# Attention normalised as it leaves PSUM, own banks for the last output parts, and scores ahead of the last image sums

## The chip, the cores and the metric

The kernel runs on one core of a Trainium2 chip. The metric is the device time of one execution in microseconds (us), as a median of several. Beside it stands the span of one profiled execution, which is some 2 us shorter than the time of the same execution.

## The reference

Spatial-reduction attention is followed by a gated feed-forward layer. The image `kv` (4 x 384 x 32 pixels of 128 channels) is averaged over 4 x 4 pixels and projected to 768 keys per batch, which are the values too. The feed-forward layer has two products of width 1536.

```python
k = v = kv_pool.reshape(B, -1, C) @ w_sr
a = softmax(q @ k.transpose(0, 2, 1) / sqrt(C))      # B=4, N=12288, C=128
x = (a @ v).reshape(B * N, C)
out = (maximum(x @ w_gate, 0) * (x @ w_val)) @ w_out  # 128 -> 1536 -> 128
```

If x is scaled by s per row, both factors of the last line are, and the output by s squared. Both kernels use that.

## The kernel before

The 49152 rows are worked in 96 tiles of 512. In a tile there are six score products and exponentials, 24 small products for the attention's output (with a column of ones beside the values, which gives the sums), 12 value products, 12 gate products, and 12 sets of 4 output products. Attention runs ahead of the feed-forward part by three tiles, and the work of both is interleaved in 12 steps per tile. Every PSUM tile is one of eight banks; what TensorE writes goes to PSUM, the other tiles lie in SBUF. In the names of tiles below, `aT` are the exponentials, `x` the attention output, `val` and `hT` the value factor and the gated product, `o_sb` the output, `rinv` the reciprocal sums. The attention output stays unnormalised, and the output is scaled by the square of the reciprocal sums:

```python
def keep_values(k, half, copy=nc.vector.tensor_copy, now=True):
    own = slice(2 * half, 2 * half + 2)
    x_ps = x_banks.pop((k, half))
    copy(x16s[k][:, own, :], x_ps[:, :, 0:C])            # L205
    sums[k, half] = x_ps[:, :, C]
    if now:
        keep_sums(k, half)

def keep_sums(k, half):
    nc.vector.reciprocal(rinvs[k][:, 2 * half : 2 * half + 2], sums.pop((k, half)))   # L211
    if half == 0:
        return
    ...
    nc.vector.tensor_tensor(inv2s[k][:, :, 0], rinv, rinv, op=ALU.mult)               # L216

# out_scale: ScalarE with inv2 as pointer, 4 of 128x128, or VectorE:
    nc.vector.tensor_tensor(o_sbs[k][:, own, :], o_banks[k][:, own, :],
        inv2s[k][:, own].to_broadcast([128, own.stop - own.start, 128]), op=ALU.mult)  # L274

# out_last: one bank for the four parts of the last tile
    o_banks[k] = bank([128, NS, 128])
    ...   # parts 0 and 1, scaled and stored together; then parts 2 and 3, one by one

# first full tile (k == LAG): ScalarE copies four half tiles out
    values(kV, jc, half)
    if jc == NJC - 1:
        keep_values(kV, half, nc.scalar.copy)
```

At the start, the last third of the image is summed and transposed (L153) before the scores of the second third:

```python
project(0, 1)
turn_open(0, 2)
turn_add(0, 2, s2, first=True)       # transposes of the first two rows' sums
for k in range(GRP):
    for jc in range(2, 4):
        scores(k, jc)
    ...
    if k == 1:                       # sums of the last two rows, and their transposes
        for h in range(2):
            s2 = add_lines(2, 2, nc.vector, slice(h, h + 1))
            turn_add(0, 2, s2, final=True, chunks=[h])
```

The softmax here doesn't subtract the row's maximum and nothing guards it: scores larger than these inputs give would overflow.

Of the kernel before, what the change touches and what calls it, by code (L numbers as in the profile page):

```python
# [9 lines left out]
FP32 = mybir.dt.float32  # L10
FP16 = mybir.dt.float16
AF = mybir.ActivationFunctionType
ALU = mybir.AluOpType
# [3 lines left out]
def kernel(  # L17
# [22 lines left out]
    nc = tc.nc  # L40

    B, N, C = q.shape
# [6 lines left out]
    NFB = D_FF // 128  # L49
    T = 512  # L50
    NS = T // 128
# [2 lines left out]
    GRP = 4  # L54
    NG = NT // GRP
    LAG = GRP - 1
    qk_scale = 1.0 / math.sqrt(C)

    assert C == 128 and N % T == 0 and J == 128 * NJC and D_FF == 128 * NFB
# [3 lines left out]
    work = ctx.enter_context(tc.tile_pool(name="work", bufs=2))  # L63
    psum = ctx.enter_context(tc.tile_pool(name="psum", bufs=8, space=bass.MemoryType.PSUM))

    def bank(shape, dtype=FP32):
        return psum.tile(shape, dtype, tag="bank", name="bank_ps")
# [50 lines left out]
    kv16 = const.tile([128, B, NJC, 2 * C + 4], FP16)  # L118
# [26 lines left out]
    def turn_open(b, pair):  # L145
        kv_Ts[b, pair] = bank([128, 2, 128])
# [27 lines left out]
        nc.vector.tensor_copy(kv16[:, b, 2 * pair : 2 * pair + 2, C : 2 * C], vt)  # L174


    aTs, x_banks, x16s, xTs, rinvs, inv2s, sums = {}, {}, {}, {}, {}, {}, {}
    hTs, o_banks, o_sbs, vals = {}, {}, {}, {}

    def scores(k, jc):  # L180
# [6 lines left out]
    def values(k, jc, half):  # L187
        if jc == 0:
            x_banks[k, half] = bank([128, 2, C + 1])
            if half == 0:  # L190
                x16s[k] = work.tile([128, NS, C], FP16, tag="x16", bufs=3, name="x16")
                rinvs[k] = work.tile([128, NS], FP32, tag="rinv", bufs=3, name="rinv")
        x_ps = x_banks[k, half]
        for i in range(2):
            s = 2 * half + i
            nc.tensor.matmul(  # L196
                x_ps[:, i, :], aTs[k][:, jc, s * 128 : (s + 1) * 128],
                kv16[:, k // NST, jc, C : 2 * C + 1],
                start=(jc == 0 and i == 0), stop=(jc == NJC - 1), skip_group_check=True,
            )  # L200

    def keep_values(k, half, copy=nc.vector.tensor_copy, now=True):
        own = slice(2 * half, 2 * half + 2)
        x_ps = x_banks.pop((k, half))
        copy(x16s[k][:, own, :], x_ps[:, :, 0:C])  # L205
        sums[k, half] = x_ps[:, :, C]
        if now:
            keep_sums(k, half)

    def keep_sums(k, half):  # L210
        nc.vector.reciprocal(rinvs[k][:, 2 * half : 2 * half + 2], sums.pop((k, half)))  # L211
        if half == 0:
            return
        rinv = rinvs.pop(k)
        inv2s[k] = work.tile([128, NS, 1], FP32, tag="inv2", bufs=8, name="inv2")
        nc.vector.tensor_tensor(inv2s[k][:, :, 0], rinv, rinv, op=ALU.mult)  # L216

    def x_turn(k):
        x16 = x16s.pop(k)
# [32 lines left out]
        if fb == NFB - 1:  # L252
            xTs.pop(k)

    def out_add(k, fb, s, first):
        nc.tensor.matmul(  # L256
            o_banks[k][:, s, :], hTs[k][:, fb, s * 128 : (s + 1) * 128], wo16[:, fb, :],
            start=first, stop=(fb == NFB - 1), skip_group_check=True,
        )

    def out_proj(k, fb):
        if fb == 0:
            o_banks[k] = bank([128, NS, 128])
        for s in range(NS):
            out_add(k, fb, s, fb == 0 and s == 0)

    def out_scale(k, engine, own):
        if k not in o_sbs:
            o_sbs[k] = work.tile([128, NS, 128], FP32, tag="o_sb", bufs=3, name="o_sb")
        if engine is nc.scalar:  # L270
            for s in range(own.start, own.stop):
                nc.scalar.mul(o_sbs[k][:, s, :], o_banks[k][:, s, :], inv2s[k][:, s])
        else:
            nc.vector.tensor_tensor(  # L274
                o_sbs[k][:, own, :], o_banks[k][:, own, :],
                inv2s[k][:, own].to_broadcast([128, own.stop - own.start, 128]), op=ALU.mult,
            )

    def out_store(k, own):
        nc.sync.dma_start(  # L280
            out[k // GRP * GRP * T : (k // GRP + 1) * GRP * T, :].rearrange(
                "(p i s) c -> i p s c", p=128, i=GRP
            )[k % GRP][:, own], o_sbs[k][:, own],
        )
        if own.stop == NS:
            for tiles in (hTs, o_banks, inv2s, o_sbs):
                del tiles[k]

    def out_last(k):
        o_banks[k] = bank([128, NS, 128])  # L290
        for s in range(2):
            for fb in range(NFB - 1):
                out_add(k, fb, s, fb == 0 and s == 0)
        for s in range(2):
            out_add(k, NFB - 1, s, False)
        out_scale(k, nc.vector, slice(0, 2))
        out_store(k, slice(0, 2))
        for s in range(2, NS):
            for fb in range(NFB):
                out_add(k, fb, s, False)  # L300
            out_scale(k, (nc.scalar, nc.vector)[s % 2], slice(s, s + 1))
        out_store(k, slice(2, NS))

    ctx.enter_context(tc.manual_schedule())
# [6 lines left out]
    make_identity(nc, ident)  # L311
    ident16 = const.tile([128, 128], FP16)
    nc.gpsimd.tensor_copy(ident16, ident)
    nc.gpsimd.memset(kv16[:, :, :, 2 * C : 2 * C + 4], 1.0)

    w_sr_f32 = const.tile([128, C], FP32)
    nc.sync.dma_start(w_sr_f32, w_sr)
# [8 lines left out]
    wo16 = const.tile([128, NFB, 128], FP16)  # L326
# [46 lines left out]
    for h in range(2):  # L373
        s2 = add_lines(1, 2, nc.vector, slice(h, h + 1))
# [3 lines left out]
    s2 = add_lines(2, 0, nc.vector, slice(1, 2))  # L378
# [5 lines left out]
    nc.gpsimd.dma_start(wo16, moe_w_out.rearrange("(fb f) c -> f fb c", f=128))  # L384
    q_load(2)
    project(0, 1)
    turn_open(0, 2)
    turn_add(0, 2, s2, first=True)
    for k in range(GRP):
        for jc in range(2, 4):  # L390
            scores(k, jc)
        if k == 0:
            turn_values(0, 1)
        if k == 1:
            for h in range(2):
                s2 = add_lines(2, 2, nc.vector, slice(h, h + 1))
                turn_add(0, 2, s2, final=True, chunks=[h])
        if k == 2:
            project(0, 2)
# [6 lines left out]
        scores(1, jc)  # L406
    attend(0, 2)
    for half in range(2):
        keep_values(0, half, now=False)
    for jc in range(4, NJC):  # L410
        scores(2, jc)
    x_turn_pe(0)
    for half in range(2):
        keep_sums(0, half)
    for jc in range(4, NJC):
        scores(3, jc)
    attend(1, 2)
    for half in range(2):
        keep_values(1, half)
    for jc in range(NJC - 2):  # L420
        values(2, jc, 0)
# [3 lines left out]

    last = NT + LAG - 1
    for k in range(LAG, last + 1):
        g, ph = divmod(k, GRP)
        if ph == 1:
            q_turn(g + 1)  # L430
            q_load(g + 2)
        b = k // NST + 1
        at = k % NST - (NST - NJC - 6)
        for step in range(NFB):
            kO, kF = k - LAG - 1, k - LAG
            half, i = divmod(step // 2, NJC // 2)
            if 0 <= kO:
                out_proj(kO, step)
                if step == NFB - 1 and k < last:
                    out_scale(kO, nc.vector if kF < NT - 2 else nc.scalar, slice(0, NS))  # L440
                    out_store(kO, slice(0, NS))
            if kF < NT:
                value_proj(kF, step)
            if k == LAG:
                own, left = left[:2], left[2:]
                for kV, jc, half in own:
                    values(kV, jc, half)
                    if jc == NJC - 1:
                        keep_values(kV, half, nc.scalar.copy)
                        if half == 1:  # L450
                            x_turn(kV)
            elif step % 2 == 0:
                if k < NT:
                    scores(k, step // 2)
            elif k > GRP and k - 1 < NT:
                values(k - 1, 2 * i, half)
                values(k - 1, 2 * i + 1, half)
                if i == NJC // 2 - 1:
                    keep_values(k - 1, half)
                    if half == 1:  # L460
                        x_turn(k - 1)
            if kF < NT:
                gate_proj(kF, step)
            if k == LAG and step == 2:
                x_turn_pe(1)
            if b < B:
                if step == 1 and 0 <= at < NJC and at % 2 == 0:
                    kv_load(b, at // 2)
                if step == 3 and 0 <= at - 2 < NJC:
                    pool_pixels(nc.gpsimd, b, (at - 2) // 2, at % 2)  # L470
                pair = (at - 5) // 2
                if at % 2 == 1 and 0 <= pair < NJC // 2:
                    if step == 2:
                        turn_open(b, pair)
                        turn_add(b, pair, s3s.pop((b, pair))[:, :, None], True, True)
                    if step == 4:
                        project(b, pair)
                    if step == 8:
                        turn_values(b, pair)
    out_scale(last - LAG - 1, nc.scalar, slice(0, NS))  # L480
    out_store(last - LAG - 1, slice(0, NS))
# [31 lines left out]
```

## Time and profile before

The first three runs gave 1050.52 us as their median.

| engine | busy us | share of the span |
|---|---|---|
| TensorE | 1035.6 | 99% |
| VectorE | 920.5 | 88% |
| ScalarE | 909.5 | 87% |
| GpSimd | 107.8 | 10% |

TensorE bounds the kernel. So the useful way is to cut the span at three TensorE instructions that both kernels have: the first value product, the first score of the next stage, and the last value product. Lines of the timeline of before (start us, duration us, engine, line, operation, out<-in):

```profile
32.81 0.38 PE L235 MATMUL bank_ps<-xT,wv 128*128 128x512 f16 x1
...
40.91 0.38 PE L184 MATMUL bank_ps<-qT,kv 128*128 128x512 f16 x1
...
1040.22 0.38 PE L235 MATMUL bank_ps<-xT,wv 128*128 128x512 f16 x1
```

This makes four stretches: start (to 32.81), first full tile (40.91 - 32.81 = 8.10), steady stage (1040.22 - 40.91 = 999.31) and tail (1048.8 - 1040.22 = 8.58). The groups by line that the change replaces (busy us, mean ns, then idle time before them):

```profile
L205 DVE CAST x<-bank_ps 128x256 f16<-128x256 f32 x188 | 77.7, 414 | 0.9 <-PE bank_ps L196 0.8
L274 DVE TENSOR_TENSOR o_sb<-bank_ps,inv 128x512 f32<-128x512 f32 x93 | 63.2, 680 | 0.0
```

### The profile page before, as it was taken

The numbers are of one execution on the slowest core, as the hardware profiler recorded it, in microseconds if no ns is written. First come the engines' busy times: TensorE is split into PE (matmuls) and PEld (weight loads), VectorE is DVE, ScalarE is ACT, GpSimd is POOL, SyncE is SP. The second block draws the span as 40 slices with busy tenths as digits, with TensorE's granted clock in tenths as the row PEclk, the third lists the DMA queues.
The fourth block names the chain that finished last, engine by engine and source line by source line (L and its number), as shares of the span: only waits on it lengthen the run. The fifth ranks groups of instructions, "written<-read, shape, count | busy, mean of one in ns | idle before, by whom it ended". The sixth has DMA issues, their size and how long they took to land.

```text
span 1048.8 us, 26047 instructions
## 1 busy us (share of the span) xinstructions
PE 1035.6 (99%) x9980; PEld 688.8 (66%) x9980; DVE 920.5 (88%) x1776; ACT 909.5 (87%) x1743; POOL 107.8 (10%) x127
## 2 busy tenths in 40 slices
PE   7999999999999999999999999999999999999998
PEld 5666666666666666666666666666666666666665
DVE  3888889898989898988989898989888888989897
ACT  2988888888888888888888888888888888888886
POOL 2000045100000015400000003430000000000000
PEclk9999999999999999999999999999999999999999
DMA  8833356241322345523224144551331322212111
GB/s 298 132 71 83 81 176 157 51 87 32 87 56 62 71 129 143 152 52 71 67 51 87 32 86 132 151 147 47 72 78 41 77 60 56 62 34 64 32 46 47
DMA packets 125853, 90.75 MB, mean 87 GB/s; under 512 B 103328, under 2 KB 104224, under 8 KB 125728
## 3 DMA queue, kind: packets, MB, share of 16 engines
q1 hardware_dynamic: 120288, 75.85, 26.7%
q0 software_dynamic: 5440, 13.24, 7.8%
q8 instruction: 78, 1.28, 0.5%
q14 instruction: 47, 0.39, 0.1%
HBM read 52.76 MB, written 25.17 MB: 74 GB/s over the span
## 4 chain that ended last, share of the span: by engine, by line
PE 96%; DMA 2%; DVE 1%; issue 0%; SPq 0%; POOL 0%; ACT 0%; DVEq 0%; POOLq 0%
PE bank_ps L256 24%; PE bank_ps L246 24%; PE bank_ps L235 24%; PE bank_ps L196 12%; PE bank_ps L184 11%; DMA parts<-in_kv_dram 2%; DVE hT L249 1%; PE bank_ps L165 0%; PE bank_ps L153 0%; POOL kv_s L345 0%; SPq L127 0%; ACT aT L185 0%; PE bank_ps L173 0%; DVE x L205 0%; DVE o_sb L274 0%
## 5 line engine op out<-in xcount | busy, mean ns | idle before, releaser
L249 DVE SCALAR_TENSOR_TENSOR hT<-bank_ps,val 128x512 f16<-128x512 f32 x1152 | 764.3, 686 | 98.0 <-ACT val L239 66.6
L239 ACT CAST val<-bank_ps 128x512 f16<-128x512 f32 x1152 | 677.3, 589 | 113.9 <-PE bank_ps L235 110.7
L256 PEld LDWEIGHTS <-hT 128*128 128x128 f16 x4608 | 351.4, 98 | 203.6 <-issue 4.0
L256 PE MATMUL bank_ps<-wo,hT 128*128 128x128 f16 x4608 | 443.5, 219 | 1.2 <-DVE o_sb L274 0.5
L246 PE MATMUL bank_ps<-xT,wg 128*128 128x512 f16 x1152 | 435.7, 378 | 1.7 <-DVE hT L249 1.7
L235 PE MATMUL bank_ps<-xT,wv 128*128 128x512 f16 x1152 | 436.6, 379 | 0.0
L185 ACT ACTIVATE aT<-bank_ps 128x512 f16<-128x512 f32 x576 | 344.9, 603 | 18.5 <-PE bank_ps L184 18.5
L196 PE MATMUL bank_ps<-kv,aT 128*128 128x129 f16 x2304 | 223.3, 219 | 0.0
L196 PEld LDWEIGHTS <-aT 128*128 128x128 f16 x2304 | 177.3, 98 | 68.4 <-issue 0.4
L184 PE MATMUL bank_ps<-qT,kv 128*128 128x512 f16 x576 | 216.2, 379 | 0.6 <-ACT aT L185 0.4
L246 PEld LDWEIGHTS <-wg 128*128 128x128 f16 x1152 | 111.4, 97 | 65.4
L235 PEld LDWEIGHTS <-wv 128*128 128x128 f16 x1152 | 112.7, 98 | 0.1
L205 DVE CAST x<-bank_ps 128x256 f16<-128x256 f32 x188 | 77.7, 414 | 0.9 <-PE bank_ps L196 0.8
L77 POOL DMA_DIRECT2D q<-in_q_dram x23 | 12.5, 545 | 569.5 <-DMA qT<-q 569.3
L274 DVE TENSOR_TENSOR o_sb<-bank_ps,inv 128x512 f32<-128x512 f32 (+1 forms) x95 | 64.0, 673 | 2.7 <-PE bank_ps L256 2.7
L136 POOL TENSOR_TENSOR s<-parts 128x512 f32<-128x512 f32 x36 | 45.3, 1270 | 165.1 <-DMA parts<-in_kv_dram 123.8
L184 PEld LDWEIGHTS <-kv 128*128 128x128 f16 x576 | 56.0, 98 | 1.6 <-issue 0.5
L211 DVE RECIPROCAL rinv<-bank_ps 128x2 f32<-128x2 f32 x192 | 30.4, 159 | 0.7 <-ACT x L205 0.6
L138 POOL TENSOR_TENSOR s<-s 128x512 f32<-128x512 f32 x18 | 22.8, 1269 | 1.4
L216 DVE TENSOR_TENSOR inv<-rinv 128x4 f32<-128x4 f32 x96 | 19.3, 201 | 3.3
L140 POOL TENSOR_TENSOR c<-s 128x256 f32<-128x256 f32 x18 | 13.1, 727 | 1.4
L160 DVE COPY kvT<-bank_ps 128x256 f32<-128x256 f32 x12 | 5.0, 416 | 6.7 <-PE bank_ps L153 6.7
(38 smaller groups left out, 88.0 us busy)
## 6 DMA issues: line engine op xcount, KB each, us to landing
parts<-in_kv_dram SPq DMA_DIRECT2D x48, 512.0 KB, 6.3
out_dram<-o_sb SPq DMA_DIRECT2D x95, 256.0 KB, 2.2
q<-in_q_dram POOLq DMA_DIRECT2D x23, 512.0 KB, 5.1
xT<-x SPq DMA_TRANSPOSE x94, 2.5
q<-in_q_dram SPq DMA_DIRECT2D x1, 768.0 KB, 8.4
wv<-in_moe_w_val_dram POOLq DMA_DIRECT2D x2, 192.0 KB, 4.3
wg<-in_moe_w_gate_dram POOLq DMA_DIRECT2D x2, 192.0 KB, 5.2
wo<-in_moe_w_out_dram POOLq DMA_DIRECT2D x1, 384.0 KB, 10.7
```

What stands on the lines that cost most here:

```text
L136: eng.tensor_tensor(s2[:, i], parts[:, 2 * i, h], parts[:, 2 * i + 1, h], op=ALU.add)
L184: nc.tensor.matmul(s_ps, kv16[:, k // NST, jc, 0:C], qT_of(k), start=True, stop=True)
L185: nc.scalar.activation(aTs[k][:, jc, :], s_ps, AF.Exp, scale=qk_scale)
L196: nc.tensor.matmul(x_ps[:, i, :], aTs[k][:, jc, s * 128 : (s + 1) * 128], kv16[:, k // NST, jc, C : 2 * C + 1], start=(jc == 0 and i == 0) ...
L205: copy(x16s[k][:, own, :], x_ps[:, :, 0:C])
L211: nc.vector.reciprocal(rinvs[k][:, 2 * half : 2 * half + 2], sums.pop((k, half)))
L235: nc.tensor.matmul(va_ps, wv16[:, fb * 128 : (fb + 1) * 128], xTs[k], start=True, stop=True)
L239: nc.scalar.copy(val, va_ps)
L246: nc.tensor.matmul(g_ps, wg16[:, fb * 128 : (fb + 1) * 128], xTs[k], start=True, stop=True)
L249: nc.vector.scalar_tensor_tensor(hTs[k][:, fb, :], g_ps, 0.0, vals.pop((k, fb)), op0=ALU.max, op1=ALU.mult)
L256: nc.tensor.matmul(o_banks[k][:, s, :], hTs[k][:, fb, s * 128 : (s + 1) * 128], wo16[:, fb, :], start=first, stop=(fb == NFB - 1), skip_gr ...
L274: nc.vector.tensor_tensor(o_sbs[k][:, own, :], o_banks[k][:, own, :], inv2s[k][:, own].to_broadcast([128, own.stop - own.start, 128]), op= ...
```

## The change

Its intent: normalise x once, as it leaves PSUM (times 512, by putting 1/512 in the column of ones, so that small averages stay well inside fp16). The squares then fall away and the output scale is a constant. Beside it, the last tile's parts get banks of their own, and scores go ahead of the last image sums.

```diff
-    def keep_values(k, half, copy=nc.vector.tensor_copy, now=True):
-        copy(x16s[k][:, own, :], x_ps[:, :, 0:C])
     def keep_sums(k, half):
-        (reciprocal, and after the second half the square into inv2s)
+        rinvs[k, half] = work.tile([128, 2, 1], FP32, tag="rinv", bufs=4, name="rinv")
+        nc.vector.reciprocal(rinvs[k, half], x_banks[k, half][:, :, C : C + 1])
+    def keep_values(k, half, engine=nc.vector):
+        if engine is nc.scalar:
+            for i in range(2):
+                nc.scalar.mul(x16s[k][:, 2 * half + i, :], x_ps[:, i, 0:C], rinv[:, i])
+        else:
+            nc.vector.tensor_tensor(x16s[k][:, 2 * half : 2 * half + 2, :], x_ps[:, :, 0:C],
+                rinv.to_broadcast([128, 2, C]), op=ALU.mult)
 ... out_scale
-            (per-row scale: 4 x nc.scalar.mul with inv2s, or tensor_tensor with inv2s)
+            nc.scalar.mul(o_sb, o_ps, 1.0 / X_SCALE**2)
+            nc.vector.tensor_scalar(o_sb, o_ps, 1.0 / X_SCALE**2, None, op0=ALU.mult)
 ... out_last
-        o_banks[k] = bank([128, NS, 128])
+        o_ps = bank([128, 2, 128])                  # parts 0 and 1
         for s in range(2, NS):
+            o_ps = bank([128, 1, 128])              # one each for parts 2 and 3
 ... start
-    turn_open(0, 2)
-    turn_add(0, 2, s2, first=True)
     for k in range(GRP):
         ...
         if k == 1:
+            turn_open(0, 2)
+            turn_add(0, 2, s2, first=True)
 ... first full tile
-                        keep_values(kV, half, nc.scalar.copy)
+                        keep_sums(kV, half)
+                        keep_values(kV, half, nc.scalar)
```

More of the change, by code (lines that the diff above doesn't have):

```diff
@@ L56 @@
     LAG = GRP - 1
+    X_SCALE = 512.0
     qk_scale = 1.0 / math.sqrt(C)
@@ L174, in turn_values @@
         nc.vector.tensor_copy(kv16[:, b, 2 * pair : 2 * pair + 2, C : 2 * C], vt)
-    aTs, x_banks, x16s, xTs, rinvs, inv2s, sums = {}, {}, {}, {}, {}, {}, {}
+    aTs, x_banks, x16s, xTs, rinvs = {}, {}, {}, {}, {}
     hTs, o_banks, o_sbs, vals = {}, {}, {}, {}
@@ L191, in values @@
                 x16s[k] = work.tile([128, NS, C], FP16, tag="x16", bufs=3, name="x16")
-                rinvs[k] = work.tile([128, NS], FP32, tag="rinv", bufs=3, name="rinv")
         x_ps = x_banks[k, half]
@@ L200, in values @@
             )
-    def keep_values(k, half, copy=nc.vector.tensor_copy, now=True):
-        own = slice(2 * half, 2 * half + 2)
-        x_ps = x_banks.pop((k, half))
-        copy(x16s[k][:, own, :], x_ps[:, :, 0:C])
-        sums[k, half] = x_ps[:, :, C]
-        if now:
-            keep_sums(k, half)
-    def keep_sums(k, half):
-        nc.vector.reciprocal(rinvs[k][:, 2 * half : 2 * half + 2], sums.pop((k, half)))
-        if half == 0:
-            return
-        rinv = rinvs.pop(k)
-        inv2s[k] = work.tile([128, NS, 1], FP32, tag="inv2", bufs=8, name="inv2")
-        nc.vector.tensor_tensor(inv2s[k][:, :, 0], rinv, rinv, op=ALU.mult)
+    def keep_sums(k, half):
+        rinvs[k, half] = work.tile([128, 2, 1], FP32, tag="rinv", bufs=4, name="rinv")
+        nc.vector.reciprocal(rinvs[k, half], x_banks[k, half][:, :, C : C + 1])
+    def keep_values(k, half, engine=nc.vector):
+        x_ps, rinv = x_banks.pop((k, half)), rinvs.pop((k, half))
+        if engine is nc.scalar:
+            for i in range(2):
+                nc.scalar.mul(x16s[k][:, 2 * half + i, :], x_ps[:, i, 0:C], rinv[:, i])
+        else:
+            nc.vector.tensor_tensor(
+                x16s[k][:, 2 * half : 2 * half + 2, :], x_ps[:, :, 0:C],
+                rinv.to_broadcast([128, 2, C]), op=ALU.mult,
+            )
     def x_turn(k):
@@ L253, in gate_proj, with out_add @@
             xTs.pop(k)
-    def out_add(k, fb, s, first):
+    def out_add(k, fb, s, o_ps, first):
         nc.tensor.matmul(
-            o_banks[k][:, s, :], hTs[k][:, fb, s * 128 : (s + 1) * 128], wo16[:, fb, :],
+            o_ps, hTs[k][:, fb, s * 128 : (s + 1) * 128], wo16[:, fb, :],
             start=first, stop=(fb == NFB - 1), skip_group_check=True,
@@ L264, in out_proj, with out_scale @@
         for s in range(NS):
-            out_add(k, fb, s, fb == 0 and s == 0)
-    def out_scale(k, engine, own):
+            out_add(k, fb, s, o_banks[k][:, s, :], fb == 0 and s == 0)
+    def out_scale(k, engine, own, o_ps=None):
         if k not in o_sbs:
             o_sbs[k] = work.tile([128, NS, 128], FP32, tag="o_sb", bufs=3, name="o_sb")
+        o_sb, o_ps = o_sbs[k][:, own], o_ps if o_ps is not None else o_banks[k]
         if engine is nc.scalar:
-            for s in range(own.start, own.stop):
-                nc.scalar.mul(o_sbs[k][:, s, :], o_banks[k][:, s, :], inv2s[k][:, s])
-        else:
-            nc.vector.tensor_tensor(
-                o_sbs[k][:, own, :], o_banks[k][:, own, :],
-                inv2s[k][:, own].to_broadcast([128, own.stop - own.start, 128]), op=ALU.mult,
-            )
+            nc.scalar.mul(o_sb, o_ps, 1.0 / X_SCALE**2)
+        else:
+            nc.vector.tensor_scalar(o_sb, o_ps, 1.0 / X_SCALE**2, None, op0=ALU.mult)
     def out_store(k, own):
@@ L285, in out_store @@
         if own.stop == NS:
-            for tiles in (hTs, o_banks, inv2s, o_sbs):
+            for tiles in (hTs, o_banks, o_sbs):
                 del tiles[k]
     def out_last(k):
-        o_banks[k] = bank([128, NS, 128])
+        o_banks[k] = None
+        o_ps = bank([128, 2, 128])
         for s in range(2):
             for fb in range(NFB - 1):
-                out_add(k, fb, s, fb == 0 and s == 0)
+                out_add(k, fb, s, o_ps[:, s], fb == 0 and s == 0)
         for s in range(2):
-            out_add(k, NFB - 1, s, False)
-        out_scale(k, nc.vector, slice(0, 2))
+            out_add(k, NFB - 1, s, o_ps[:, s], False)
+        out_scale(k, nc.vector, slice(0, 2), o_ps)
         out_store(k, slice(0, 2))
         for s in range(2, NS):
+            o_ps = bank([128, 1, 128])
             for fb in range(NFB):
-                out_add(k, fb, s, False)
-            out_scale(k, (nc.scalar, nc.vector)[s % 2], slice(s, s + 1))
+                out_add(k, fb, s, o_ps[:, 0], fb == 0)
+            out_scale(k, (nc.scalar, nc.vector)[s % 2], slice(s, s + 1), o_ps)
         out_store(k, slice(2, NS))
@@ L313 @@
     nc.gpsimd.tensor_copy(ident16, ident)
-    nc.gpsimd.memset(kv16[:, :, :, 2 * C : 2 * C + 4], 1.0)
+    nc.gpsimd.memset(kv16[:, :, :, 2 * C : 2 * C + 4], 1.0 / X_SCALE)
     w_sr_f32 = const.tile([128, C], FP32)
@@ L408 @@
     for half in range(2):
-        keep_values(0, half, now=False)
+        keep_sums(0, half)
+    for half in range(2):
+        keep_values(0, half)
     for jc in range(4, NJC):
@@ L412 @@
     x_turn_pe(0)
-    for half in range(2):
-        keep_sums(0, half)
     for jc in range(4, NJC):
@@ L418 @@
     for half in range(2):
+        keep_sums(1, half)
         keep_values(1, half)
@@ L458 @@
                 if i == NJC // 2 - 1:
+                    keep_sums(k - 1, half)
                     keep_values(k - 1, half)
```

## The prediction

> **What bounds the kernel now.** I read four views of the kernel before, in this order: busy time per engine, TensorE's waits, the timeline around each wait, and the histories of single groups. The first two (of a wait: total us, times, longest):
>
> ```profile
> PE 1035.6 (99%) x9980; PEld 688.8 (66%) x9980; DVE 920.5 (88%) x1776; ACT 909.5 (87%) x1743; POOL 107.8 (10%) x127
> ...
> PE bank_ps L246 <- DVE hT L249: 1.7, 4, 0.5
> ...
> PE bank_ps L256 <- DVE o_sb L274: 0.5, 1, 0.5
> PE bank_ps L256 <- ACT o_sb L272: 0.5, 1, 0.5
> ```
>
> TensorE is busy for 1035.6 of 1048.8 us, so all its gaps are 13.2 us, 1.3% of the span. In the timeline of a steady stretch a 128x512 matmul starts 0.215 us after the one before it and a set of four 128x128 ones takes 0.22 us: TensorE streams without pause, at a granted clock of 0.999. VectorE and ScalarE have about a tenth of each tile free. The change removes no matmul, so it can only win some of the 13.2 us: four stalls by VectorE (1.7), the start, and the last 8 us.
>
> The four stalls lie at 157, 391, 646 and 668 us, and each has the same neighbours. Timeline at the first (start, duration), then the history of the small multiply L216 (min/median/max ns):
>
> ```profile
> 155.83 0.16 DVE L211 RECIPROCAL rinv<-bank_ps 128x2 f32<-128x2 f32 x1
> 156.02 1.14 DVE L216 TENSOR_TENSOR inv<-rinv 128x4 f32<-128x4 f32 x1
> ...
> 155.87 1.27 POOL L136 TENSOR_TENSOR s<-parts 128x512 f32<-128x512 f32 x1 [2.29 <-DMA parts<-in_kv_dram]
> ...
> L216 DVE TENSOR_TENSOR inv<-rinv x96: 161/163/1178, 32.3 to 1026.4; 128x4 f32<-128x4 f32 x96
> ```
>
> The 0.16 us multiply takes 1.14 us and ends 0.02 us after the GpSimd add (155.87 + 1.27 = 157.14). At 390, 645 and 667 us it takes 0.96, 1.18 and 1.13 us, beside the same GpSimd line. The hT behind it frees its bank late, and TensorE's next gate product stands still for 0.46 us.
>
> **What the Trainium skill says.** "SBUF — State Buffer", section "Who interferes with whom": a VectorE instruction with two SBUF inputs contends with a GpSimd one that reads SBUF, and the second to start blocks fully; with at most one SBUF input, outside the two-port modes, it does not. The trace agrees on both sides: L216 has two SBUF inputs and stretched to 1.18 us, while L249 and L274, each with one PSUM and one SBUF input, never exceed 0.693 and 0.682 us. "VectorE: DVE Perf Modes", "Why PSUM operands drop a tier": fp32 from PSUM runs at the base rate. So the multiply out of PSUM should cost what the cast costs; here a 128x256 multiply of L274's kind took 0.425 us and the cast L205 0.414. "ScalarE: Activation LUTs", "What ACT_TABLE_LOAD costs": a per-partition pointer operand adds some 93 ns. Here four 128x128 scalings with a pointer (L272) take 1.15 us, a spacing of 0.26, no cheaper than one 128x256 cast (spacing 0.27). "PSUM — Partial Sum Buffer", "PSUM bank collisions raise a hardware error": two engines in one bank are kept apart by semaphores even at different columns. The trace agrees: TensorE waits for the scaling of other columns of the last output bank.
>
> **The change, part by part.**
>
> *Squares removed.* 96 L216 go, and with them the only two-SBUF-input VectorE instruction of the steady stage. Normalising replaces cast (0.33 to the next start) and reciprocal. Before, the half tile with the square cost 0.33 + 0.19 + 0.08 = 0.60 us of VectorE, the other 0.33 + 0.08 = 0.41. After, each costs 0.20 (reciprocal, then a dependent start) + 0.34 = 0.54. The sum per tile goes from 1.01 to 1.08: VectorE gets no freer. But the half that follows the 0.60 us output scaling, where the slack is smallest, becomes 0.06 shorter and can't stretch; the other grows 0.13, beside gaps of 0.28 us. So all four stalls go: **-1.7 us**.
>
> *Constant output scale.* The 128x512 scaling out of PSUM stays a base-rate pass, 0.68 us: 0. On ScalarE, four scalings (1.15) become one of about 0.59, only for two tiles at the end.
>
> *Start.* In the order before, keys are ready at 21.63 us, but TensorE sits in front of the moved transposes:
>
> ```profile
> 21.21 0.42 DVE L166 TENSOR_SCALAR kv<-bank_ps 128x256 f16<-128x256 f32 x1
> ...
> 22.32 1.10 PE L153 MATMUL bank_ps<-ident,kv_s 128*128 128x128 f32 x8 [1.14 <-POOL kv_s L345]
> ...
> 23.25 0.59 PE L184 MATMUL bank_ps<-qT,kv 128*128 128x512 f16 x2
> ```
>
> After, scores start at 21.70, the value copy is done at 23.03 instead of 24.28, VectorE's two image sums start at 23.0 (24.20 before), the transposes end near 25.1 instead of 26.2, and the rest follows: -1.1. The image rows don't hold it up: the DMA rate falls from 418 to 49 GB/s by 22.0-22.5, so they have landed. Against it, tile 0's first transposes wait for two reciprocals before the casts' successors, +0.2. **-0.9 us**.
>
> *First full tile (33 to 40 us).* Here ScalarE copies four half tiles in between value casts:
>
> ```profile
> 35.90 0.38 ACT L205 CAST x<-bank_ps 128x256 f16<-128x256 f32 x1
> ...
> 36.31 0.17 DVE L211 RECIPROCAL rinv<-bank_ps 128x2 f32<-128x2 f32 x1
> ```
>
> Before, the reciprocal followed at leisure. After, ScalarE must wait for it, and it stands in VectorE's queue behind the previous step's hT. The second half tile thus starts at 36.5 instead of 35.9 and occupies 0.52 instead of 0.27. Carried on with these durations (casts 0.48, hT 0.61 apart): the third half tile starts at 39.1 instead of 37.9, the fourth at 41.6 instead of 39.9, so ScalarE is 1.9 us late. Eight banks hide part of it. In the built order the bank of the third half tile is reused by the gate product of step 9, due at 39.4 and free at 39.7; step 11's value product waits 0.3 more; the first score of the next stage reuses the fourth half tile's bank, due at 41.7 after those stalls and free at 42.25. Sum of stalls **+1.4 us** (0.35 + 0.3 + 0.1 + 0.6). The next stage can't win it back: from 40 to 50 us ScalarE is busy for 10.00 of 10.00 us.
>
> *Tail.* Last output, before:
>
> ```profile
> 1043.06 0.83 PE L256 MATMUL bank_ps<-wo,hT 128*128 128x128 f16 x12 [0.52 <-DVE o_sb L274]
> ...
> 1044.35 0.83 PE L256 MATMUL bank_ps<-wo,hT 128*128 128x128 f16 x12 [0.46 <-ACT o_sb L272]
> ...
> 1045.28 0.29 DVE L274 TENSOR_TENSOR o_sb<-bank_ps,inv 128x128 f32<-128x128 f32 x1 [2.28 <-PE bank_ps L256]
> ```
>
> With own banks the two sets of 12 (0.66 us apart) follow the first part at once: that part ends at 1042.54, so a next set can start at 1042.37; the second of the two ends at 1042.37 + 0.66 + 0.83 = 1043.86 and the last scaling starts at 1043.95 instead of 1045.28: -1.3. The shorter ScalarE scaling of the last tile but two takes away a 0.53 us gap of VectorE at 1034, of which some 0.2 reach the end. **-1.5 us**.
>
> Sum: -1.7 - 0.9 + 1.4 - 1.5 = -2.7, and 1050.52 - 2.7 = 1047.8 us.
>
> **The rivals.** (1) VectorE load goes down by 96 x 0.2 = 19 us and the kernel by much of it. Against: TensorE's rows leave no gap per tile to win, and VectorE idles 0.28 us again and again for ScalarE's casts. It would give 1031; I hold it for nearly excluded. (2) Banks and engines absorb the first full tile, for instance because the reciprocal comes early enough; then the +1.4 falls away: 1046.4. For it: I chose every duration and start by hand, and some waits above are within 0.1 us of vanishing. But the next queries limit it: their transpose, issued at 32.91, takes 7.2 us to land (40.1), and their first score stood at 40.91, so at most 0.8 of the early gain passes. (3) The later reciprocal-multiply pair, 0.13 longer in the first half, delays a bank each tile: 96 x 0.1 would give 1057 instead. Against: the stretched L216 added 0.98 us and cost only 0.46, so over 0.4 us is slack even at the tightest place. (4) The start is held by the image rows or queries: -0.9 becomes 0, giving 1048.7.
>
> **Range and chances.** The sizes are sure for the stalls and tail (together -3.2, within 0.5), unsure for start and first tile (their sum +0.5, anywhere from -0.8 to +1.5). Runs before spread by 1.5 us. So 1046.0 to 1049.8. Two per cent is 21 us, more than all gaps of TensorE: faster or slower than that is nearly excluded.
>
> **What would show it.** Right: no TensorE wait for hT near 157, 391, 646, 668; normalising multiplies at about 0.43 us beside GpSimd adds too; VectorE busy still within 10 us of 920; the first scores of the second keys near 21.7; TensorE waits of 0.3 to 0.6 us for ScalarE between 39 and 42 us; the last scaling about 1.3 us sooner after the previous part than now. Wrong: a multiply that stretches with GpSimd, new hT waits once per tile, or a tail whose final store, 3.2 us from its issue at 1045.60 to the end, grows.

## The result

The changed kernel took 1048.24 us (median of six, 1047.74 to 1049.42) against 1050.37. The ratio is 0.9979 (95% interval 0.9966 to 0.9992). The profiled span fell from 1048.8 to 1046.4 us, by 2.4. The first line below is from the page of the changed kernel, with busy time per engine:

```profile
PE 1036.4 (99%) x9980; PEld 691.1 (66%) x9980; DVE 913.8 (87%) x1680; ACT 908.5 (87%) x1741; POOL 107.6 (10%) x127
```

The bound is the same, and VectorE lost 6.7 us of busy time, not 19, though its count fell by 96. Two lines of TensorE's waits in the changed kernel (line, waited for: total us, times, longest):

```profile
PE bank_ps L154 <- DVE kv_s L343: 1.6, 2, 1.1
...
PE bank_ps L185 <- ACT x L210: 0.4, 1, 0.4
```

The wait of the gate product for hT is gone, and so are both waits of the last outputs for o_sb. Of the two lines shown, the first lies in the start and has grown from 0.9 us (the transposes of the image sums wait for VectorE's sums), and the second is new (a score waits for ScalarE's x to free a bank). Most of what TensorE loses shows in the spacing of its starts. The same three cuts in the timeline of the changed kernel:

```profile
32.82 0.38 PE L234 MATMUL bank_ps<-xT,wv 128*128 128x512 f16 x1
...
42.33 0.38 PE L185 MATMUL bank_ps<-qT,kv 128*128 128x512 f16 x1 [0.36 <-ACT x L210]
...
1039.40 0.38 PE L234 MATMUL bank_ps<-xT,wv 128*128 128x512 f16 x1
```

| stretch | before | after | difference | predicted |
|---|---|---|---|---|
| start | 32.81 | 32.82 | 0.0 | -0.9 |
| first full tile | 8.10 | 9.51 | +1.4 | +1.4 |
| steady stage | 999.31 | 997.07 | -2.2 | -1.7 |
| tail | 8.58 | 7.00 | -1.6 | -1.5 |
| span | 1048.8 | 1046.4 | -2.4 | -2.7 |

The total came out as the sum of one term that failed, one too small and two right. The groups that took the place of the cast and the scaling (same columns as before):

```profile
L212 DVE TENSOR_TENSOR x<-bank_ps,rinv 128x256 f16<-128x256 f32 x188 | 79.7, 424 | 6.7 <-DVE rinv L204 0.2
L273 DVE TENSOR_SCALAR o_sb<-bank_ps 128x512 f32<-128x512 f32 x93 | 63.2, 680 | 0.0
```

The normalising multiply costs 0.424 us where the cast cost 0.414, and none of the 188 took more than 0.426; the output scaling costs 0.680 us with a constant as with a per-row factor. Now the start, in the timeline of the changed kernel:

```profile
24.00 1.29 DVE L343 TENSOR_TENSOR kv_s<-parts 128x512 f32<-128x512 f32 x2 [1.62 <-DMA parts<-in_kv_dram]
```

VectorE was ready for the last image sums 1.62 us earlier, but the rows were not there. The kernel before began the same sums at 24.20 without a wait for rows:

```profile
24.20 1.28 DVE L345 TENSOR_TENSOR kv_s<-parts 128x512 f32<-128x512 f32 x2
```

The tail, in the timeline of the changed kernel:

```profile
1039.84 2.99 PE L255 MATMUL bank_ps<-wo,hT 128*128 128x128 f16 x48
...
1042.87 0.29 DVE L273 TENSOR_SCALAR o_sb<-bank_ps 128x128 f32<-128x128 f32 x1 [0.91 <-PE bank_ps L255]
```

The last output products are one run, with no wait for o_sb in it. The last scaling comes 1042.87 - 1039.40 = 3.47 us after the last value product, against 1045.28 - 1040.22 = 5.06 before.

### The profile page after: what moved, and what is told of

It reads as the page before. It is cut to its first block, busy times and chain, and to the rows that moved or that the text cites. A ratio compares the mean times of both kernels' runs of the same rounds, so it can differ in the third digit from the quotient of the medians.

```text
span 1046.4 us, 25971 instructions
## 1 busy us (share of the span) xinstructions
PE 1036.4 (99%) x9980; PEld 691.1 (66%) x9980; DVE 913.8 (87%) x1680; ACT 908.5 (87%) x1741; POOL 107.6 (10%) x127
## 4 chain that ended last, share of the span: by engine, by line
PE 97%; DMA 2%; SPq 0%; DVE 0%; ACT 0%; issue 0%; DVEq 0%; ACTq 0%
PE bank_ps L255 25%; PE bank_ps L234 24%; PE bank_ps L245 24%; PE bank_ps L196 12%; PE bank_ps L185 12%; DMA parts<-in_kv_dram 1%; DMA q<-in_q_dram 1%; PE bank_ps L166 0%; PE bank_ps L154 0%; SPq L128 0%; ACT val L238 0%; PE bank_ps L174 0%; PE bank_ps L227 0%; DVE kv_s L343 0%; DVE rinv L204 0%
## 5 line engine op out<-in xcount | busy, mean ns | idle before, releaser
L212 DVE TENSOR_TENSOR x<-bank_ps,rinv 128x256 f16<-128x256 f32 x188 | 79.7, 424 | 6.7 <-DVE rinv L204 0.2
L273 DVE TENSOR_SCALAR o_sb<-bank_ps 128x512 f32<-128x512 f32 (+1 forms) x95 | 64.0, 673 | 1.3 <-PE bank_ps L255 1.3
L154 PE MATMUL bank_ps<-ident,kv_s 128*128 128x128 f32 x50 | 7.8, 275 | 1.6 <-DVE kv_s L343 1.6
```

Of the source, the lines that this page charges most:

```text
L212: nc.vector.tensor_tensor(x16s[k][:, 2 * half : 2 * half + 2, :], x_ps[:, :, 0:C], rinv.to_broadcast([128, 2, C]), op=ALU.mult,)
L273: nc.vector.tensor_scalar(o_sb, o_ps, 1.0 / X_SCALE**2, None, op0=ALU.mult)
```

## The experiments

The theory after the result has four parts. (a) The four stalls before came from the small multiply with two SBUF inputs, locked out by GpSimd. (b) The loss in the first full tile is ScalarE standing in front of reciprocals. (c) The start is held by image rows that land near 24 us in either order. (d) The tail's gain is the banks. The rivals stand in the expectations. Because the landing of the rows moves the start by up to 1.2 us from run to run, verdicts are read from the four stretches of each profile, and the times are given beside them.

### again: the changed kernel once more

No edit but a comment.

> The changed kernel once more, beside the others of this set. Every theory: about 2.1 us faster than before (ratio 0.998), no TensorE wait for hT after 100 us, the first score of the second stage near 42.3 us (40.9 before), the final image sums started near 24.0 us by the landing of image rows.

It took 1048.31 us against 1050.02, ratio 0.9983. Stretches: 33.16, 9.52, 997.08, 7.04. The last three repeat within 0.04 us; the start moved by 0.34, with the sums at 24.34.

### squares_psum: the kernel before, its squares with one input in PSUM

```diff
-        nc.vector.tensor_tensor(inv2s[k][:, :, 0], rinv, rinv, op=ALU.mult)
+        nc.vector.tensor_tensor(inv2s[k][:, own, 0], rinvs[k][:, own], x_sums, op=ALU.mult)
```

It runs once for each half tile. The result is not the square, so the output is wrong.

> The kernel before, its small multiply given one SBUF and one PSUM input instead of two SBUF inputs (output wrong on purpose), one for each half tile. My theory (the two SBUF inputs were locked out by the GpSimd adds): no multiply over 0.25 us, the four TensorE waits for hT gone, span shorter by 2.2 us (four times a matmul pitch of some 0.8 instead of 0.215), about 1046.6 of 1048.8. Rival (the stalls come from the amount of VectorE work at that place): the multiplies add 0.08 us per tile, the stalls stay, span as before within 0.3 us.

It took 1048.51 us, ratio 0.9986, as fast as the changed kernel. Stretches: 32.93, 8.18, 997.05, 8.54. The steady stage has all of the gain (999.31 before, 997.07 changed) and the other stretches are those of before. The history of the multiply (min/median/max ns):

```profile
L215 DVE TENSOR_TENSOR inv<-rinv,bank_ps x192: 156/157/158, 32.3 to 1024.3; 128x2 f32<-128x2 f32 x192
```

There are twice as many multiplies as before, and the longest took 158 ns instead of 1178. The amount of VectorE work was not the cause.

### dummy_sbuf and dummy_psum: a small multiply put back

In the changed kernel, behind each normalising multiply on VectorE, with its result unused:

```diff
+            sq = work.tile([128, 2, 1], FP32, tag="sq", bufs=4, name="sq")
+            nc.vector.tensor_tensor(sq, rinv, rinv, op=ALU.mult)                       # dummy_sbuf
+            nc.vector.tensor_tensor(sq, x_ps[:, :, C : C + 1], rinv, op=ALU.mult)      # dummy_psum
```

> The changed kernel with a small multiply of two SBUF inputs put back behind each normalising multiply, its result unused. My theory: most of these take 0.16 us but some, beside a GpSimd add, 0.5 to 1.3 us; 4 to 12 of 188 stretch, several TensorE waits for hT come back, span longer than the changed kernel by 1 to 4 us. Rival: all take 0.16 us and the span is the same within 0.3 us.

> The same with one of the two inputs in PSUM (the sums' column). My theory: none over 0.25 us, no TensorE wait for hT after 100 us, span within 0.3 us of the changed kernel's 1046.4. Rival (any further small VectorE instruction there costs it): the same loss as with two SBUF inputs.

With two SBUF inputs it took 1055.10 us (1051.53 to 1055.72), ratio 1.004; with one of them in PSUM 1048.39, ratio 0.9985. Steady stages: 1004.00 and 997.06 us. So in the steady stage 188 small instructions cost nothing in one form and 6.9 us in the other. The multiply's history in dummy_sbuf, then in dummy_psum:

```profile
L217 DVE TENSOR_TENSOR sq<-rinv x188: 149/151/2744, 30.4 to 1032.2; 128x2 f32<-128x2 f32 x188
```

```profile
L217 DVE TENSOR_TENSOR sq<-bank_ps,rinv x188: 148/150/152, 31.4 to 1026.3; 128x2 f32<-128x2 f32 x188
```

The loss was larger than I expected (1 to 4 us). In the trace 12 of the 188 stretched, as expected, to between 0.34 and 2.74 us; but three of them lasted over two GpSimd adds (1.70, 2.74 and 2.68 us), where I had expected at most 1.3. The group's busy time is 41.9 us, 13.5 more than 188 x 0.151. Timeline of dummy_sbuf at the worst place, by engine:

```profile
418.12 2.74 DVE L217 TENSOR_TENSOR sq<-rinv 128x2 f32<-128x2 f32 x1
420.78 2.47 DVE L250 SCALAR_TENSOR_TENSOR hT<-bank_ps,val 128x512 f16<-128x512 f32 x4
...
417.75 0.57 POOL L78 DMA_DIRECT2D q<-in_q_dram  x1
418.34 2.49 POOL L137 TENSOR_TENSOR s<-parts 128x512 f32<-128x512 f32 x2
...
421.52 0.38 PE L185 MATMUL bank_ps<-qT,kv 128*128 128x512 f16 x1 [1.69 <-DVE hT L250]
```

The multiply begins while GpSimd issues a transfer, and ends at 420.86, 0.03 us after the second of two adds that run back to back (418.34 + 2.49 = 420.83). It was not let in between them. That is the exception: seven of the 12 met two adds back to back, and four of these ended with the first. TensorE then stood for 1.69 us.

### scale_later and scale_split: the first full tile

The four scalings on ScalarE are moved behind the next step's value cast (scale_later), and in scale_split the first and last of them go to VectorE too:

```diff
+                for kV, half in due:
+                    keep_values(kV, half, nc.scalar)     # scale_split: nc.vector for (2, 0) and (3, 1)
+                    if half == 1:
+                        x_turn(kV)
+                due = []
                 for kV, jc, half in own:
                     values(kV, jc, half)
                     if jc == NJC - 1:
                         keep_sums(kV, half)
-                        keep_values(kV, half, nc.scalar)
-                        if half == 1:
-                            x_turn(kV)
+                        due.append((kV, half))
```

> The changed kernel, ScalarE's scaling of the four half tiles in the first full tile moved behind the next step's value cast, so that the reciprocal is long done. My theory (the loss of 1.4 us there is mostly ScalarE standing for reciprocals, three times about 0.5 us, the rest 4 x 0.25 us of longer scaling): no ScalarE wait for rinv, first score of the second stage at 41.2 to 41.6 us instead of 42.3, span 0.7 to 1.1 us shorter than the changed kernel. Rival (the loss is the longer scaling alone): 42.3 stays within 0.2 us, and so does the span.

> The same, and the first and the last of the four half tiles scaled on VectorE. My theory: ScalarE has 2 x 0.25 us less to do than with all four, nothing is left of the loss: first score of the second stage at 40.9 to 41.1 us, span 1.2 to 1.5 us shorter than the changed kernel, the fastest so far near 1045.0. Rival (VectorE is as full as ScalarE there, hT runs late instead): no better than with the scaling moved alone.

Timeline of ScalarE in the changed kernel, where the number in brackets is its idle time:

```profile
36.59 0.62 ACT L210 ACTIVATE x<-bank_ps,rinv 128x128 f16<-128x128 f32 x2 [0.57 <-DVE rinv L204]
37.10 1.56 ACT L238 CAST val<-bank_ps 128x512 f16<-128x512 f32 x3
39.12 0.63 ACT L210 ACTIVATE x<-bank_ps,rinv 128x128 f16<-128x128 f32 x2 [0.46 <-DVE rinv L204]
39.63 1.56 ACT L238 CAST val<-bank_ps 128x512 f16<-128x512 f32 x3
41.65 0.62 ACT L210 ACTIVATE x<-bank_ps,rinv 128x128 f16<-128x128 f32 x2 [0.46 <-DVE rinv L204]
```

And in scale_later:

```profile
36.75 0.62 ACT L210 ACTIVATE x<-bank_ps,rinv 128x128 f16<-128x128 f32 x2
37.27 1.56 ACT L238 CAST val<-bank_ps 128x512 f16<-128x512 f32 x3
38.69 0.66 ACT L210 ACTIVATE x<-bank_ps,rinv 128x128 f16<-128x128 f32 x2
```

ScalarE no longer stands. Scale_later took 1047.08 us against 1050.04, ratio 0.9969; its stretches are 32.93, 8.10, 997.01, 7.06. The whole 1.4 us came back, more than the 0.7 to 1.1 that I had expected: the three waits, 0.57 + 0.46 + 0.46 = 1.49 us, were the loss, and the longer scaling itself cost nothing visible. Scale_split took 1047.23 us, ratio 0.9972, with stretches 32.20, 8.11, 997.01, 6.98. Its lower span, 1044.3 against 1045.1, is the earlier start of that one profile (its rows were there at 23.39 us); in the first full tile it wins nothing further, as nothing was left to win. So the first score at 40.31 is no merit of the split.

### order_back, rows_landed and rows_landed_back: the start

Order_back puts `turn_open` and the first `turn_add` back ahead of the loop. The other two add the first two rows of the last third twice, so that the last sums need no late rows; their output is wrong.

```diff
+        at = 0 if pair == 2 else dh
-            s2[:, chunks], line(pair, dh)[:, chunks], line(pair, dh + 1)[:, chunks], op=ALU.add
+            s2[:, chunks], line(pair, at)[:, chunks], line(pair, at + 1)[:, chunks], op=ALU.add
```

> The changed kernel with the scores back behind the image sums, as before. The prediction's step said the order wins 1.1 us. My theory now (the final sums wait for image rows that land near 24.0 us in either order): first full tile begins within 0.3 us of the changed kernel's 32.8, span within 0.4 us of it. Rival (the prediction's): 1.1 us longer.

> The changed kernel, where the last image sums of the start add the first two rows of their pair twice, so that they need not wait for the last two rows (output wrong on purpose). My theory (in the changed order the start waits for those rows and for nothing else): sums start at 22.2 to 22.7 us instead of 24.0 to 24.5, first full tile at 31.0 to 31.6 instead of 32.8 to 33.4, the kernel shorter by 1.0 to 1.8 us than the changed one, unless the transposed second queries (landing near 40 us) take part of it back. Rival (something else in the start holds it): 32.2 or later.

> The same in the old order of scores and sums. My theory: without the rows the old order's own limit shows: sums start near 24.0 to 24.3 us as in the kernel before, first full tile at 32.7 to 33.1, so the order is worth 1.1 to 1.8 us once the rows are there. Rival: the same start as in the new order, the order is worth nothing.

| run | time us | ratio | last sums start | first full tile begins |
|---|---|---|---|---|
| order_back (old order) | 1048.76 | 0.9987 | 24.30 | 33.11 |
| rows_landed (new order) | 1047.39 | 0.9976 | 22.73 | 31.78 |
| rows_landed_back (old order) | 1048.68 | 0.9988 | 24.41 | 33.22 |

The sums' line in the timeline of rows_landed, then of rows_landed_back:

```profile
22.73 1.28 DVE L344 TENSOR_TENSOR kv_s<-parts 128x512 f32<-128x512 f32 x2
```

```profile
24.41 1.28 DVE L344 TENSOR_TENSOR kv_s<-parts 128x512 f32<-128x512 f32 x2
```

With the rows' wait away, the new order begins the tile 33.22 - 31.78 = 1.44 us sooner than the old one. With the wait, it is worth only what the rows leave: the old order's sums start by its own limit at 24.2 to 24.4, and the rows land near there. In the seven profiles of the new order with the rows' wait (changed, again, dummy_sbuf, dummy_psum, scale_later, scale_split, one_bank), the sums started between 23.39 and 24.54 and the tile began 8.8 to 8.9 us later each time, so between 32.20 and 33.43, 32.75 on average. Against the 33.11 of order_back that is some 0.4 us, and order_back's five spans, 1046.9 us on average, stand against 1046.4 over the eleven of the changed kernel, from other rounds. So the order wins a little where the rows are early; one pair of profiles does not show it. Rows_landed started a little later than I expected (31.78 against at most 31.6): its sums were at 22.73, and the tile followed 9.05 us later, as TensorE was still at the transposes before theirs (16 in one run, 23.06 to 24.97). Rows_landed_back was some 0.1 us later than I expected in both columns.

When the rows landed in the old order, which did not wait for them, the packet records in the kept traces tell; no view lists them one by one. In the changed kernel the last seven 4 KB packets of the rows' queue run one at a time, from 22.13 to 23.45 us, and the sums begin 0.55 us after the last; in the other six profiles of that order it is 0.53 to 0.55. In the kernel before the last packet ends at 23.42, so I estimate that its rows were there by 23.97, before its own 24.20; in order_back by 24.31, just as its sums began. The stretches of the changed kernel (last two columns: mean busy share of the 16 DMA engines, GB/s) agree:

```profile
22.00:22.50 0.50, 0.36 (x3) 0.01 (x1) 0.29 (x1) 0.50 (x2) 0.50 (x2) 1.00 0.07 16
22.50:23.00 0.50, 0.50 (x5) 0.50 (x5) 0.00 (x0) 0.50 (x2) 0.50 (x2) 1.00 0.06 25
```

A share of 0.06 is that of one engine in 16. Why one is late, no run shows.

### one_bank: the last tile's parts in one bank again

```diff
-        o_ps = bank([128, 2, 128])
+        whole = bank([128, NS, 128])
+        o_ps = whole[:, 0:2]
-            o_ps = bank([128, 1, 128])
+            o_ps = whole[:, s : s + 1]
             for fb in range(NFB):
-                out_add(k, fb, s, o_ps[:, 0], fb == 0)
+                out_add(k, fb, s, o_ps[:, 0], False)
```

> The changed kernel with the last tile's parts in one bank again. My theory: the two TensorE waits for o_sb of 0.5 us come back, last scaling 1.3 us later (within 0.15), span 1.3 us longer. Rival (the shorter ScalarE scaling made the tail): under 0.5 us longer.

It took 1049.68 us, ratio 0.9993. Stretches: 32.30, 9.52, 997.08, 8.30. Of TensorE's waits, these two are back:

```profile
PE bank_ps L255 <- DVE o_sb L273: 0.5, 1, 0.5
PE bank_ps L255 <- ACT o_sb L271: 0.4, 1, 0.4
```

The tail is 8.30 us instead of 7.00: the own banks are 1.3 of the 1.6 us, and 8.58 - 8.30 = 0.28 is the rest of the change, which I put down to the shorter scaling on ScalarE (that was not tried by itself). The span is only 0.8 us above the changed kernel's because this profile's start was 0.5 us earlier.

## Why the prediction was right or wrong

The predicted 1047.8 stands beside a measured 1048.24, inside the range. By its steps:

- **What bounds the kernel: right.** TensorE is at 99% in both, and only its gaps moved.
- **Squares removed, -1.7: right in mechanism, too small.** Squares_psum shows the cause, with 2.26 us for the same change of operands alone. The term was mis-sized because I summed the idle time that the list of waits gives. Idle starts at a matmul's modelled end, 0.38 us after its start, while the next one in an unbroken stream starts after 0.215. Each stall thus costs 0.38 - 0.215 = 0.165 more than its idle time: 1.7 + 4 x 0.165 = 2.36, near the 2.24 seen. At the first stall the starts were 157.81 and 156.98, so 0.83 instead of 0.215. By the same account that stall cost 0.62 us and not 0.46, so the slack that the third rival was weighed with was under 0.4.
- **VectorE's load per tile: right.** The step said that it gets no freer, with busy time within 10 us of 920: it is 913.8. The pair of reciprocal and multiply caused no wait of TensorE after the start, so the third rival fell.
- **Constant output scale, 0: right.** 0.680 us before and after on VectorE; on ScalarE one of 0.60 in place of four in 1.15. A 128x128 one there took 0.277 us with the constant and 0.374 with the pointer, which agrees with the 93 ns that the prediction cites.
- **Start, -0.9: wrong.** The step that failed is "The image rows don't hold it up: the DMA rate falls from 418 to 49 GB/s by 22.0-22.5, so they have landed." The scores did move ahead (the first at 21.33 us, predicted 21.7). But the rows landed at 24.0 in the changed kernel, and between 23.4 and 24.5 in six more profiles of its order. A falling rate says that most of the bytes are there; a sum waits for the last of them. In the profile of before, the two halves of the stretch from 22.5 to 23.5 still moved 25 and 16 GB/s, near a sixteenth of 400, and the last seven packets ran one at a time until 23.42. Rows_landed and rows_landed_back show that the order would have won 1.44 us otherwise. The fourth rival is what happened; that it came out at 0.0 us is partly chance, as the tile of the new order began anywhere from 32.20 to 33.43 us. The smaller part of the step, reciprocals ahead of tile 0's transposes at +0.2, was right: from the last sums' start to the first full tile 8.61 us before and 8.82 after. In these two profiles the reordering won the sums 0.2 us (24.20 to 24.00), and the two cancel.
- **First full tile, +1.4: right.** 1.41 in the profile; the second half tile was scaled at 36.59 (predicted 36.5), the third at 39.12 (39.1), the fourth at 41.65 (41.6). TensorE's starts are late by 0.23 us at 39.79, 0.27 at 40.76 and 0.52 at 42.33 (predicted 0.35, 0.3 and 0.6), the rest in pieces of about 0.1. That the next stage can't win it back was right too. What the step had as a part, the scaling's longer occupation, costs nothing by itself, as scale_later shows. Rival 2 fell.
- **Tail, -1.5: right.** 1.58, of which 1.3 by the banks.

So the small error of the total, 0.3 us in the span, hides an error of 0.9 in one term and of 0.5 in another that went against it; that they met was luck. Without the cuts into stretches the sum would have looked better than its working was.

A version that beats both kernels came out of the experiments: the changed kernel with ScalarE's four scalings one step later (scale_later), 0.9969 of before against 0.9979 and 0.9983 for the changed kernel. The two were not timed in the same rounds, but the slowest of its five runs (1047.28 us) lies below the fastest of the changed kernel's eleven (1047.74). Whether scale_split (0.9972) is any better is not decided by these runs, and by its stretches it isn't.

## What to carry to other kernels

When one engine is busy 99% of the time, list its gaps and price a change by them alone; price a stall by the distance of two starts, not by the idle time that the waits give. A cross-engine wait put into an in-order queue costs the position that the producer has in its own queue: emit the consumer one step later, and here it was free. A transfer has landed when something that waits for it says so; a falling rate says only that most of it has.

## What the Trainium skill lacked or had wrong

- "SBUF — State Buffer", "Who interferes with whom", says that issue order decides who blocks on the ports that VectorE and GpSimd share. The contention itself is as it says. But a multiply of two SBUF inputs that began at 418.12 us, 0.22 before two GpSimd adds and during a GpSimd transfer issue (417.75 to 418.32), ended only after both adds, at 420.86: 2.74 us for an instruction of 0.15. At 676.25 us one took 2.68 in the same situation, and one that began inside the first of two adds, at 162.31, took 1.70 and ended with the second; four others in that place ended with the first. The page says nothing of a waiting instruction that is passed over between two adds.
- The same page infers that a two-input multiply doesn't meet descriptor generation. The two multiplies at 418.12 and 676.25 began inside a transfer's issue. At 0.15 us, the first would have ended at 418.27, before the issue did (418.32) and before the add began (418.34), and it did not: a hint that the issue held it, from one case and times of GpSimd that are rough. No run here tests it.
- No page gives a size for how far the last DMA engine of a load can lag behind the others (it belongs to "DMA: Bandwidth & Descriptors"). In the changed kernel the rate was 74 GB/s at 21.5 to 22.0 us and 16 at 22.0 to 22.5, after about 400; the last packets ran one at a time until 23.45, and the rows were there at 24.0.
